# A new hand-set order for the 2,475 operations of a two-branch kernel (S4D convolution beside Hedgehog linear attention)

## The chip, the cores and the metric

The kernel runs on one core of a Trainium2 chip. Its time is the device time of one execution in microseconds (us). The engines are PE (TensorE: matrix products into PSUM), DVE (VectorE), ACT (ScalarE), POOL (GpSimd) and SP (SyncE, which issues all DMA transfers here). Each engine works through its own queue in order.

## The reference

Two independent branches read their own inputs, and their results stand side by side in the output (2048 rows, 576 + 576 columns).

```python
# A: S4D convolution.  u: 2048 x 576, 128 states per channel
dt = exp(log_dt);  A = -exp(log_A_real) + 1j * A_imag;  C = (C_real + 1j * C_imag) * dt
P = exp((A * dt)[:, :, None] * pos)                    # 576 x 128 x 2048
K = 2 * einsum("dn,dnl->dl", C, P).real                # the convolution's kernel
y = irfft(rfft(u, 4096) * rfft(K, 4096))[:2048] + u * D_skip
# B: linear attention, 32 heads of 18.  x: 2048 x 576
q, k, v = x @ wqkv;  pq, pk = q @ w_phi, k @ w_phi     # w_phi per head
phi = concat(softmax(p), softmax(-p))                  # for q and for k
o = phi_q (phi_k^T v) / (phi_q sum(phi_k) + 1e-6);  out = o @ wo
```

## The kernel before, in words

Branch A is a Fourier transform in two stages, written as small matrix products. Its steps are: `mags` and `par` (the parameters); 18 `group` units, each of two groups of 16 channels, which build the convolution's kernel; `kfirst` (first stage of the transform of the kernel, four quarters); `u` (the same for the input, 16 steps); 16 `product` units (second stage, product, and the first stage back); 16 `last` units (second stage back, and the stores). Between the stages the data goes through DRAM. A group's six PSUM tiles of sizes (step g0, PE) are exponentiated on ACT (L793), multiplied on DVE (L797 to L802), and enter the matmuls of step g4. In a product, p1 and p2 turn input and kernel on PE, DVE multiplies (L307), p3 adds on POOL or DVE, p4 turns back on PE, and two copies into `zo` buffers are stored.

Branch B folds w_phi into wq and wk (`fold`, 128 x 128 blocks), runs 16 `key` tiles of 128 rows (two products with 14 matmuls per half of the columns, softmax, and a sum over rows into one PSUM bank), turns the sum (`kv`), and runs 16 `query` tiles (product, softmax q1 and q2, transposes q3, division q4, transposes q5, product with wo q6, store). The first 8 tiles of x are kept in DRAM as `xd` by the key tiles, and loaded again by the query tiles (L400).

All operations are first recorded in `Plan.ops`, 2,475 of them, each with its engine. For some there are two engines ("any": ACT or DVE; others: POOL or DVE). `Plan.run` then emits them in the order of one list of numbers, `ORDER` (from L971). A number there can carry `x` (the other engine), `@` with the PSUM banks that the operation's new tiles take, and `:n`, which puts n matmuls of zeros (L230, 128 x 256, bf16) on PE ahead of it. Nothing else sets the order: each engine's queue is the list, cut down to that engine. An operation that has to wait (for data, for a free buffer, for a PSUM bank) holds up all that stands behind it in its queue, SP's DMAs too.

A buffer comes from a tag with a fixed number of places, given out in the order of the list. The tags that matter here: `zi`, `zo` and `v1` have 2 places, `e`, `x9`, `ot` and `ac` 3, `cs` and `ub` 5. PSUM has 8 banks, and the list says which one each tile takes; a tile of 576 columns takes two.

The places that the prediction speaks of: `load_again` (L400), the query tile's last product (step q6) and its store (L583), `product` (loads L886 and L877, stores L935), and `last`, whose load of `zi` or `cs` (L945) comes after the last store of all eight products of its half, and whose two stores (L958) free an `ot` buffer.

Of the kernel before, what the change touches and what calls it, by code (L numbers as in the profile page):

```python
# [971 lines left out]
0 1 2 4 3 5 1132 1136 1135 1124 1186 1133 34 1134 51 20 1137 35@0:26 36 39 52 21@2:10 22 37 53 1138 1139 1148 1140 1155 1141 1142 1143 1105 38 27 1144  # L972
1145 6 359 28@4 29 8@6 13 1146 32 40 1147 1149 7 25 23 1150 360 30 14@0:11 15 1106 1127 47 1151 1156 1193 44 361x 11 9 362 18 16 48 33 31 26 24 279
1152 1153 1157 1154 1158 1159 12 1160 1161 54 45 57@4 364@2 1024 1167 1168 41 1108 1128 280 1162 10 17 1163 19 363:2 1164 1109 1110 1107 49 42 281x
1035 56 376 299 1100 46 282x 1111 368 61 367 59@6 366@0 43 365 72 55 1095 1112 1125 58 1113 1116 370 1129 60 1118 369 1114 1115 371x 1117 377 1096@20
1120 62 63 1121 1122 300 70 64x 301x 73 1036@46 1098 65 284@0 1119 1037x 66 372 1126 373 1165 1166 1194 1187 1195 1188 1196 1189 1190 283 1097x 1197
1198 1038 1232 1191 74 1192 302 67 374 1123 288 287 1180 289 75x 68 306@4 375 303@6 1169 304 307 1224 177 1199 308 1201 1231 1233 1234 1090 1225 69
305 1235 1170 50@2 1226 71 378 317x 310 1179 1200 114 1099 1202 1183@30 309 1236 311 290 291 1428 1039 1203 286@4 77@6 1206 178 1171 1184@13 1204 1207
292 1212 78 293 1205 1429 1208 1215 285 1025 1030 1185@03 76 312 1209 82 1210@1 1227 1237 1228 1229 81 83 294 297 1431 179 316 115 180 182@4 181 183
1230 1238 1214 1211x 79@6 313 314 1213 1432 1218 116 117 80 295x 1172 84 1263 315x 318 186 187 1217 1216 188 1262 296 298 1173 1433 1219@3 1239 1240  # L980
85x 1221@10 1241 189 379 1269 1270 1271 1272 1264 91 1220x 1242 1244 339 340 1245 219 1181 118 86 1080 1182 119@4 90 1174 1175 1176 1430 184@6 341x
1222@31 342 198 1250 1243 1130 132 1177 1273 185 120 87 190x 1253 121@0 1178 1265 191 1274 1434 88 220 1435 124 89x 123 125 122 126 1223@45 1247 92
196 1251 1246 199 1248@3 221 1436 1437 222 133 1266 1308 1267 1252 195 127 224@6 223 1275 1268 128 1254 1256 192 1453 1452 1438 193 343@0 1249 129
1277 1276 1278 344 194x 1255 93 345@4 348 197 228 1439 130 346 227 347 229 1260@36 350 349 1281 1307 357 200 201x 1309 131x 1259@70 1279 1257@1 134
351x 1440 1441 230 226@4 94 1258 231 1288 1301 1300 1282 1285 1302 1303 95 1280 1283 1304 232 1444 225 1284 237 204@0 1305 233 203 1306 1314 96 395x
1291 1081@46 1286@3 236 1083 1082 234 235 238 1310 1261@67 352 208 207 209 210 1290 353 1289 1293 99@4 98 205@0 1311 354 1294 206 1312 1313 319 1292
1084 320 1315 211 1339 321 102 103 104 1338 356 1287 216 1316 355x 1050 1442 217 1101@64 1102x 1295@3 105 1297@01 1317 106 1340 1341 1342 1298@67 1318
97 202 1326 1346 1103x 1345 322 1296x 1320 100@4 101 1319 1323 1322 107 1070 1321 1329 259 260 1343 1344 358 1299@30 212 1352 1324@1 1347 1348 1349
1350 323@6 324 1328 108 109 1104 1351 111 110x 239 1327 1325x 112x 1331 1332 327 325@4 328 329 240 113 1443 1330 1445 261 262 1353 1071@06 326 1354
1072 1446 1073 1447 241x 213 1449 1448 242 1451 1091@06 330 337 1336@34 1092 1093 1045 1333@5 331x 1335@01 243@6 1450 214 1381 135 1454 244 1455 1456  # L990
1384 1457 1334 1074 1355 1358 156 1458 245@4 1459 1357 1361 1360 1527 1460 215x 1461 1356 1359 248 247 246 136 157 218 1362@3 249 1476 1131 257x 158
1462 332 264@0 1363 159x 1364 1365@64 1528 1529 1530 1531 263 333 1520 1482 336 1521 1522 1523 1524 1525 250 1483 256 334 1094 1366x 1367 1337@34 1368
1383 1382 268 267 251 1386 269 335x 270 1387 266@6 252 265 271 1369@04 338 1385 137 138 1370 1371 1388@3 1373@04 253 1475 1372 1374x 277 140@6 1375
1377@40 1376 1489 475 1065 272 273 274 1484 1532 1378x 141 1379x 254 1490 1491 1389x 145 144 162@4 146 161 160 1051@06 1533 1535 1526 1492 1485 1534
1486 1536 255x 276 1487 275x 258 1053 165 147 1518@36 1052x 1517@70 1537 1538 278 1054 166 168 167 396 1546 1540 142@4 1539 1541 143 1549 1075 1380
# [78 lines left out]
```

## Time and profile before

| | |
|---|---|
| median of 3 runs | 548.41 us (548.35 to 549.57) |
| the profiled execution's own time | 552.82 us |
| its span, first to last instruction | 551.0 us |
| mean granted PE clock | 0.990 |
| busy: PE, DVE, ACT, POOL | 529.0, 455.8, 378.6, 319.0 us |
| matmuls on PE | 8,048, of them 102 of zeros |
| DMA | 107.01 MB |

Rows of the profile read: line of the kernel, engine, operation, output<-inputs by the kernel's names, partitions x elements, count, and busy time with the mean of one in ns. A wait is put down to the instruction or transfer that ended it.

### The profile page before, as it was taken

The numbers are of one execution on the slowest core, as the hardware profiler recorded it, in microseconds if no ns is written. First come the engines' busy times: TensorE is split into PE (matmuls) and PEld (weight loads), VectorE is DVE, ScalarE is ACT, GpSimd is POOL, SyncE is SP. The second block draws the span as 40 slices with busy tenths as digits, with TensorE's granted clock in tenths as the row PEclk, the third lists the DMA queues.
The fourth block names the chain that finished last, engine by engine and source line by source line (L and its number), as shares of the span: only waits on it lengthen the run. The fifth ranks groups of instructions, "written<-read, shape, count | busy, mean of one in ns | idle before, by whom it ended". The sixth has DMA issues, their size and how long they took to land. (4 is left out here: it accounts for less than half of the span.)

```text
span 551.0 us, 18919 instructions
## 1 busy us (share of the span) xinstructions
PE 529.0 (96%) x8048; PEld 440.9 (80%) x8048; DVE 455.8 (83%) x762; ACT 378.6 (69%) x549; POOL 319.0 (58%) x463
## 2 busy tenths in 40 slices
PE   8999999999999889999999999978999999999997
PEld 7888999988988777888877577656879777777976
DVE  7999998979878889989999998978966878758541
ACT  4769849699468889899799987987732442533431
POOL 1645777964689877970888867884503544503200
PEclk9999999999999999999999999989799999999999
DMA  8858510263266568626662778555569788887876
GB/s 218 277 189 279 187 30 21 72 219 92 83 164 221 180 215 286 195 87 176 207 207 107 209 234 249 162 183 156 172 182 291 228 266 262 259 260 244 301 230 169
DMA packets 85650, 107.01 MB, mean 194 GB/s; under 512 B 5186, under 2 KB 69826, under 8 KB 85566
## 3 DMA queue, kind: packets, MB, share of 16 engines
q1 hardware_dynamic: 85566, 105.80, 61.6%
q8 instruction: 63, 1.03, 0.8%
q14 instruction: 21, 0.17, 0.1%
HBM read 61.24 MB, written 44.54 MB: 192 GB/s over the span
## 5 line engine op out<-in xcount | busy, mean ns | idle before, releaser
L288 PE MATMUL psum<-wh,x 128*128 128x288 f32 x576 | 123.3, 300 | 1.7 <-DMA x<-xd 0.9
L288 PE MATMUL psum<-vh,x 128*128 128x288 f32 x576 | 123.7, 302 | 1.2 <-DVE v L293 0.6
L739 POOL TENSOR_TENSOR cs<-cs,pi 128x64 int32<-128x64 int32 (+4 forms) x180 | 106.1, 596 | 9.2
L288 PEld LDWEIGHTS psum<-vh,x 128*128 128x128 f32 x576 | 94.9, 190 | 7.4 <-issue 2.9
L288 PEld LDWEIGHTS psum<-wh,x 128*128 128x128 f32 x576 | 94.2, 188 | 7.7 <-issue 2.6
L288 PE MATMUL psum<-vl,x 128*128 128x288 f32 x320 | 94.3, 297 | 0.5 <-DVE vl L376 0.5
L288 PE MATMUL psum<-wl,x 128*128 128x288 f32 x320 | 93.9, 296 | 0.1
L793 ACT ACTIVATE psum<-psum 128x512 f32<-128x512 f32 x108 | 59.0, 585 | 8.9 <-PE psum L288 8.4
L288 PEld LDWEIGHTS psum<-vl,x 128*128 128x128 f32 x320 | 60.9, 190 | 0.9 <-DVE vl L376 0.9
L288 PEld LDWEIGHTS psum<-wl,x 128*128 128x128 f32 x320 | 60.2, 188 | 0.3 <-DVE wl L360 0.3
L303 POOL TENSOR_TENSOR x<-zo,x 128x512 fp32r<-128x512 f32 (+1 forms) x34 | 31.6, 934 | 45.1 <-ACT x L387 31.6
L303 POOL TENSOR_TENSOR e<-e,small 128x1152 f32<-128x1152 f32 (+1 forms) x26 | 43.8, 1684 | 12.7 <-DVE small L307 5.6
L797 DVE TENSOR_TENSOR cs<-psum,cs 128x1024 f32<-128x1024 f32 x36 | 43.8, 1218 | 6.5 <-ACT psum L793 6.5
L288 PE MATMUL psum<-cs 128*32 128x64 f32 x2304 | 41.3, 223 | 4.5 <-issue 4.3
L798 DVE TENSOR_TENSOR cs<-psum,cs 128x1024 f32<-128x1024 f32 x36 | 43.7, 1214 | 1.2 <-ACT psum L793 0.8
L303 POOL TENSOR_TENSOR e<-small,e 128x576 f32<-128x576 f32 x22 | 25.7, 1170 | 32.5 <-DVE small L431 30.0
L288 PEld LDWEIGHTS psum<-cs 128*32 128x32 f32 x2304 | 35.0, 111 | 11.7 <-issue 7.7
L288 PE MATMUL psum<-ub,ff 64*32 64x288 f32 x1024 | 40.1, 418 | 2.5 <-ACT zo L293 0.9
L288 PEld LDWEIGHTS psum<-kvb,fT 126*128 126x128 f32 (+1 forms) x320 | 38.8, 190 | 4.6 <-issue 1.7
L293 ACT ACTIVATE zi<-psum 128x576 f32<-128x576 f32 x43 | 26.5, 651 | 23.2 <-PE psum L288 17.4
L434 ACT ACTIVATE e<-e 128x1152 f32<-128x1152 f32 x32 | 37.2, 1170 | 6.0 <-POOL e L303 4.8
L288 PE MATMUL psum<-kvb,fT 126*128 126x133 f32 (+1 forms) x320 | 41.2, 278 | 0.1
(153 smaller groups left out, 1128.3 us busy)
## 6 DMA issues: line engine op xcount, KB each, us to landing
dram<-zi SPq DMA_DIRECT2D x32, 576.0 KB, 7.2
ub<-dram SPq DMA_DIRECT2D x64, 288.0 KB, 4.0
dram<-zo SPq DMA_DIRECT2D x32, 288.0 KB, 4.4
zo<-in_xT_dram SPq DMA_DIRECT2D x24, 320.0 KB, 5.0
zi<-dram SPq DMA_DIRECT2D x12, 576.0 KB, 7.2
ub<-in_u_dram SPq DMA_DIRECT2D x16, 288.0 KB, 4.6
xd<-x SPq DMA_DIRECT2D x8, 576.0 KB, 5.2
x<-xd SPq DMA_DIRECT2D x8, 576.0 KB, 5.7
```

What stands on the lines that cost most here:

```text
L288: pe.matmul(o, l, r, start=start, stop=stop, skip_group_check=skip)
L293: op(("act", "dve"), (c_act(n), c_dve(n)), lambda e: act.activation(dst(), src(), AF.Copy) if e == "act" else dve.tensor_copy(dst(), src() ...
L303: op(eng, [c_dve(n[0]) if e == "dve" else c_pool(n[1]) for e in eng], lambda e: (dve if e == "dve" else pool).tensor_tensor(dst(), a(), b( ...
L434: op("act", c_act(1152) + 40, lambda: act.activation(e.t, e.t, AF.Exp), r=[e], w=[e], table="exp")
L739: op("pool", c_pool(2 * n * W), lambda n=n, j=j: pool.tensor_tensor(x()[:, :, :, n:2 * n], x()[:, :, :, 0:n], pi.t[:, j:j + 2, gs].bitcast ...
L793: op("act", c_act(512), lambda b=b: act.activation(b.t, b.t, AF.Exp), r=[b], w=[b], table="exp")
L797: op("dve", c_dve(64 * W), lambda: dve.tensor_tensor(F(), both(M.t), F(), op=ALU.mult), r=[M, cs], w=[cs])
L798: op("dve", c_dve(64 * W), lambda: dve.tensor_tensor(E.t[:, :, :, 32:64], both(up.t), cs.t[:, :, :, 0:32], op=ALU.mult), r=[up, cs], w=[E])
```

## The change

Only the list of numbers is new. The operations, their tiles, the tags and their places are the same. The first line of the list, before and now (89 such lines became 90):

```diff
 ORDER = """
-0 1 2 4 3 5 1132 1136 1135 1124 1186 1133 34 1134 51 20 1137 35@0:26 36 39 52 21@2:10 22 37 53 1138 1139 1148 1140 1155 1141 1142 1143 1105 38 27 1144
+0 1 2 4 3 1193 34 1132 1133 51 1135 5 35@0:13 36 39 20 21@2:22 27 1127 6 1124 22 359 1136 13 1134 1137 40 37 1138 1139 52 28@4 1140 1156 29 1141 38
...
```

Matmuls of zeros: 107 instead of 102. The start has 13 + 22 + 11 where it had 26 + 10 + 11, and a few stretches in the middle have some more or fewer. 163 operations run on their second engine instead of 160, so that DVE has one operation more, ACT two fewer, POOL one more. PE's operations are the same 481 with the same matmuls; most moves on PE are swaps of neighbours. On SP many transfers stand elsewhere. The lists also give other PSUM banks to many tiles.

Three places follow in detail. A number behind a name tells the buffers of one tag apart and differs between the two kernels.

The first is **SP's queue around the second load of x for query tile 6** (L400, `x9_4389` before, `x9_4200` now). Around it stand loads of the products (L886, L877), the stores of `u` (L608) and `kfirst` (L835), and the query tiles' result stores (L583; `ot_3912` before and `ot_3936` now are query tile 0's). Before:

```order
L886 DMA ub_4253<-dram_695 128x2x288
L886 DMA ub_4255<-dram_2390 128x2x288
L877 DMA ff_4376<-in_ff_dram 128x512
L886 DMA ub_4378<-dram_2390 128x2x288
L886 DMA ub_4380<-dram_695 128x2x288
L400 DMA x9_4389<-xd_863 128x1152
L583 DMA out_0_dram<-ot_3912 128x576
L886 DMA ub_4714<-dram_2390 128x2x288
```

Now:

```order
L400 DMA x9_3934<-xd_2845 128x1152
L835 DMA dram_2430<-zi_3948 128x8x144
L608 DMA dram_858<-zi_4025 128x1152
L583 DMA out_0_dram<-ot_3932 128x576
L400 DMA x9_4200<-xd_1091 128x1152
L608 DMA dram_858<-zi_4092 128x1152
L608 DMA dram_858<-zi_4113 128x1152
L583 DMA out_0_dram<-ot_3936 128x576
L877 DMA ff_4205<-in_ff_dram 128x512
```

The load stood behind the loads of the first products, and now stands ahead of all of them.

The second is **SP's queue in the last 30 us**. `zi_7885` before and `zi_7887` now are the load of `last` unit 12; `zi_7897` before and `zi_7810` now that of unit 8; `ot_7658` before and `ot_7651` now the result buffer of unit 1, whose second store stands here; the other `cs` and `zi` loads are those of other last units. Before:

```order
L958 DMA out_0_dram<-ot_7658 64x2x288
L945 DMA zi_7766<-dram_6780 128x1152
L958 DMA out_0_dram<-ot_7682 64x2x288
L945 DMA cs_7786<-dram_6780 128x1152
L945 DMA cs_7818<-dram_6780 128x1152
L945 DMA cs_7822<-dram_6780 128x1152
L958 DMA out_0_dram<-ot_7820 64x2x288
L583 DMA out_0_dram<-ot_7776 128x576
L958 DMA out_0_dram<-ot_7816 64x2x288
L945 DMA zi_7885<-dram_6780 128x1152
```

Now:

```order
L958 DMA out_0_dram<-ot_7673 64x2x288
L583 DMA out_0_dram<-ot_7783 128x576
L945 DMA cs_7808<-dram_6780 128x1152
L945 DMA zi_7810<-dram_6780 128x1152
L958 DMA out_0_dram<-ot_7651 64x2x288
L958 DMA out_0_dram<-ot_7856 64x2x288 x2
L945 DMA zi_7887<-dram_6780 128x1152
L583 DMA out_0_dram<-ot_7878 128x576
```

Unit 1's second store stood ahead of six of the eight loads of these units, and now stands behind seven of them. Ahead of it is unit 8's load, for which a `zi` buffer must come free.

The third is **PE's queue in the same stretch**: `zi_7766` before and `zi_7770` now is the input of last unit 10, the other `zi` that of unit 14; `o` belongs to query tile 14 and `fT` to 15; the last row is the first matmul of query tile 12's product with wo (`vh`), of which one half of the columns is done first. Before:

```order
L288 MATMUL psum_73<-zi_7766,w1_292 64x288 x4
L288 MATMUL psum_73<-zi_7759,w1_292 64x288 x4
L571 MATMUL psum_73<-ident_84,o_7764 128x128 x4
L572 MATMUL psum_73<-ident_84,o_7764 128x128
L288 MATMUL psum_73<-kvb_1048,fT_7788 128x133 x8
L288 MATMUL psum_73<-kvb_1048,fT_7788 128x76 x2
L288 MATMUL psum_73<-vh_3268,x9_7769 128x288
```

Now:

```order
L288 MATMUL psum_73<-zi_7762,w1_388 64x288 x4
L288 MATMUL psum_73<-zi_7770,w1_388 64x288 x4
L288 MATMUL psum_73<-kvb_896,fT_7801 128x133 x8
L288 MATMUL psum_73<-kvb_896,fT_7801 128x76 x2
L571 MATMUL psum_73<-ident_84,o_7781 128x128 x4
L572 MATMUL psum_73<-ident_84,o_7781 128x128
L288 MATMUL psum_73<-vh_3210,x9_7792 128x288
```

Units 10 and 14 have changed places, and the transposes went behind the division. In the list, query tile 12's product took the banks from 2 on before, in which unit 14 had its sums, and takes those from 0 on now, in which unit 10 has them.

More of the change, by code (lines that the diff above doesn't have):

```diff
@@ L976 @@
[L976 to L991, printed above, removed]
```

149 lines of the change are left out of this document (83 added, 66 removed).

## The prediction

> **What bounds the kernel now.** I began with the page's busy times and its slices.
>
> ```profile
> PE 529.0 (96%) x8048; PEld 440.9 (80%) x8048; DVE 455.8 (83%) x762; ACT 378.6 (69%) x549; POOL 319.0 (58%) x463
> PEclk9999999999999999999999999989799999999999
> ```
>
> PE is busy for 529.0 of 551.0 us, and the change leaves its matmuls as they are. Only three things can get shorter: the 22.0 us in which PE stands, what PE loses at a lowered clock, and the tail behind its last matmul. So I read what ended PE's waits (columns: us in total, times, longest).
>
> ```profile
> PE psum L288 <- issue: 4.3, 3, 2.4
> PE psum L288 <- ACT zi L293: 1.9, 2, 1.4
> ...
> PE psum L230 <- DVE zero L326: 1.5, 1, 1.5
> ...
> PE psum L288 <- DMA x<-xd: 0.9, 1, 0.9
> PE psum L288 <- DMA zi<-dram: 0.8, 1, 0.8
> PE psum L288 <- DVE v L293: 0.6, 1, 0.6
> ```
>
> There is no large wait: after the 4.3 us that are no wait for data ("issue"), each is at most 1.5 us. A new order can take away single ones of under a microsecond. Next the windows of 50 us around the places where it matters (busy us of PE, PEld, DVE, ACT, POOL, then the PE clock).
>
> ```profile
> 50.00:100.00 50.00, 50.00 (x885) 46.95 (x884) 46.40 (x70) 40.29 (x55) 39.92 (x55) 1.00 0.32 106
> ...
> 300.00:350.00 50.00, 48.59 (x954) 34.55 (x938) 47.48 (x73) 41.88 (x62) 38.53 (x58) 1.00 0.74 221
> 350.00:400.00 50.00, 44.53 (x861) 32.35 (x863) 43.65 (x63) 38.99 (x57) 33.30 (x49) 0.90 0.52 156
> ```
>
> From 50 to 100 us PE is never idle. From 300 to 350 us DVE is busy for 47.48 of 50 us, nearly as much as PE: a PE wait that an order takes away there can come back a little later, since DVE's work is the same. From 350 to 400 us the clock is 0.90, and there windows of 5 us show more.
>
> ```profile
> 365.00:370.00 5.00, 2.59 (x88) 1.36 (x82) 1.98 (x5) 4.47 (x6) 3.90 (x7) 0.90 0.51 163
> 370.00:375.00 5.00, 5.00 (x68) 3.32 (x52) 4.12 (x7) 3.10 (x4) 4.69 (x6) 0.76 0.40 114
> ...
> 385.00:390.00 5.00, 4.30 (x53) 2.96 (x55) 4.55 (x6) 3.56 (x8) 0.48 (x1) 0.61 0.96 290
> 390.00:395.00 5.00, 5.00 (x105) 4.43 (x100) 5.00 (x7) 4.19 (x8) 3.67 (x4) 0.71 0.72 217
> ```
>
> PE was busy for 2.59 of 5 us, and then had 0.90 and 0.76 of its clock; later 0.61 and 0.71. Lost clock: 5 x (0.10 + 0.24) = 1.7 us, and 5 x (0.39 + 0.29) = 3.4 us, 5.1 us in all.
>
> **The change part by part.** The sum is made against the profiled execution's 552.82 us (its span of 551.0 and 1.8 around it), and brought to the median by 548.41 / 552.82 = 0.992.
>
> *Waits removed.* In PE's timeline (start, length, and in brackets the idle time ahead):
>
> ```profile
> 48.85 0.40 PE L288 MATMUL psum<-vh,x 128*128 128x288 f32 x1 [0.64 <-DVE v L293]
> ...
> 50.79 0.30 PE L288 MATMUL psum<-wh,x 128*128 128x288 f32 x1
> ...
> 287.18 0.41 PE L288 MATMUL psum<-vh,x 128*128 128x288 f32 x1 [0.27 <-ACT ot L293]
> ...
> 290.17 0.37 PE L288 MATMUL psum<-wh,x 128*128 128x288 f32 x1 [0.86 <-DMA x<-xd]
> ...
> 310.65 1.35 PE L288 MATMUL psum<-ub,ff 64*32 64x288 f32 x32 [0.36 <-DVE o L307]
> 312.58 0.72 PE L288 MATMUL psum<-ub,ff 64*32 64x288 f32 x16 [0.57 <-ACT ac L293]
> ...
> 355.70 0.40 PE L288 MATMUL psum<-wh,x 128*128 128x288 f32 x1 [0.64 <-DVE ac L307]
> ...
> 534.53 1.19 PE L288 MATMUL psum<-zi,w 128*64 128x288 f32 x8 [0.80 <-DMA zi<-dram]
> ```
>
> And what such a load of x takes, from the DMA rows (KB, median us to landing):
>
> ```profile
> x<-xd SPq DMA_DIRECT2D x8, 576.0 KB, 5.7
> ```
>
> Query 6's product at 290.17 waited 0.86 us for x, a load of 5.7 us. The load now stands on SP ahead of all loads of the first products, for whose buffers it no longer waits; if that brings it forward by one such load, it is there in time. The same product also goes ahead of query 2's half (287.18), which had 0.27 us to wait for a bank. Removed: 1.13 us.
>
> The wait at 534.53 is `last` 12's, the load issued at 528.64 in the chain of waits:
>
> ```profile
> 527.93 0.61 SPq L958
> ...
> 528.64 5.76 DMA zi<-dram
> ...
> 547.31 0.65 ACT ot L293
> ```
>
> A `zi` load needs 5.76 us here. Unit 12 now comes after units 8, 11 and 15 as well on PE, where 9 alone was ahead of it; three more units of about 1 us (1.19 in the row at 534.53) against 0.80. Removed: 0.80 us.
>
> The key tile's product at 48.85 now has another key tile's half ahead of it (14 matmuls, 50.79 - 48.85 = 1.9 us), which covers its 0.64 us. At 355.70, query 8's first half waited 0.64 us for a bank; its second half now goes first, some 1.9 us of work. Removed: 0.64 each. Product 5's first stage (310.65, 312.58) waited 0.36 + 0.57 = 0.93 us; the third of its four turns takes another bank now, and its loads stand earlier, but one is still late by the same durations: removed 0.64 us, 0.3 left.
>
> Sum removed: 1.13 + 0.80 + 0.64 + 0.64 + 0.64 = 3.85 us. The last two (1.28) lie where DVE is nearly full; none of that need last, so the lower end is 2.6.
>
> *Waits added, the tail.* The DMA rows of the stores:
>
> ```profile
> dram<-zo SPq DMA_DIRECT2D x32, 288.0 KB, 4.4
> out_dram<-ot SPq DMA_DIRECT2D x32, 144.0 KB, 4.4
> ```
>
> Query 12's product now takes the banks of unit 10, whose copy needs the `ot` buffer of unit 1, whose second store now stands on SP behind unit 8's load, and that waits for unit 14's matmuls. From the end of those: the load's issue and the store's, 0.61 each by the chain's SPq row (the store's lies within its 4.4), 4.4 to land, 0.65 for the copy: about 5.7 us. PE has in between the other unit (about 1.1 us), query 15's division and query 14's transposes:
>
> ```profile
> 525.30 0.66 PE L571 MATMUL psum<-ident,o 128*128 128x128 f32 x4
> 525.80 0.27 PE L572 MATMUL psum<-ident,o 128*128 128x128 f32 x1
> 525.90 2.41 PE L288 MATMUL psum<-kvb,fT 126*128 126x133 f32 x20
> ```
>
> That is 1.1 + (528.12 - 525.30 =) 2.8, or 3.9 us. A stall of 1.3 to 1.8 us follows; nothing on PE can pass it. What it delays is everything to the end. Since SP's own wait may end earlier than I put it, the bounds are 0 and 1.8; I take 1.3. Behind the store on SP stand the other results' stores and unit 12's load, which has room (above).
>
> *Product 9's last step (448.87)* now takes the banks in which query 12's scores stood, and so for the last of DVE's three steps on those scores (maximum, minimum, addition):
>
> ```profile
> L307 DVE TENSOR_TENSOR e<-psum,small 128x576 f32<-128x576 f32 x32 | 24.0, 750 | 0.9 <-issue 0.5
> ```
>
> DVE has the list's order too, and the two preceding steps lie beside PE's work; bounds are 0 and one such step, 0.75, and since the step stands directly ahead of PE's in the list, I take 0.6.
>
> *Matmuls of zeros.* Five more.
>
> ```profile
> 1.46 5.73 PE L230 MATMUL psum<-ident,zero 128*128 128x256 bf16 x26 [1.46 <-DVE zero L326]
> 6.98 1.33 PE L288 MATMUL psum<-fT,kvb 72*128 72x72 f32 x10
> 8.15 1.26 PE L230 MATMUL psum<-ident,zero 128*128 128x256 bf16 x10
> 9.24 1.28 PE L288 MATMUL psum<-fT,cs 126*128 126x126 f32 x10
> ```
>
> One takes (9.24 - 8.15) / 10 = 0.109 us, and (6.98 - 1.46) / 26 = 0.212 us at the start, where the clock is still low. Five: 0.55 us, if they don't fall into a wait. The start itself: 13 cold ones end at 4.2 us, the first block, whose load now stands second on SP, takes 1.3 to 2, and 22 more, of which the last some 15 are warm, end near 9.2. Before it was 9.24 us: nothing.
>
> *Sum:* -3.85 + 1.3 + 0.6 + 0.55 = -1.4 us, from 552.82 to 551.4, and by 0.992 to **547.0 us**. With the ends named: -3.85 + 0.55 = -3.3 (545.1), and -2.6 + 1.8 + 0.75 + 0.55 = +0.5 (548.9).
>
> *What I leave at nothing:* the "issue" waits.
>
> ```profile
> q8 instruction: 63, 1.03, 0.8%
> ...
> 368.88 0.22 PE L288 MATMUL psum<-cs 128*32 128x64 f32 x1 [2.41 <-issue]
> ```
>
> 63 instruction packets for 8,048 matmuls and as many weight loads are one for every 255 or 256 of PE's instructions; the three waits stand 256 or a multiple apart in PE's count, in stretches of many small matmuls. Ten instructions more hardly move the marks: they still fall there, so the 2.41 us may grow, shrink or stay. The Trainium skill ("Runtime: NRT & Kernel Launch", Instruction fetch mechanics) says that an engine's instructions come in blocks of 256 and that crossing a border is mostly hidden. The count agrees with this trace, and the 2.41 us show a crossing that isn't hidden; by the rule alone 4.3 us would be a chance of this execution, and no order would owe them.
>
> **The rivals.**
>
> *More than the sum.* The idle 2.4 us before 369, and the low clock after it, may vanish together when the marks and the waits around 380 fall otherwise. Price: 2.41 of idle and 1.7 of clock at 369, less what DVE takes back, so about 3 us more: 551.4 - 3 = 548.4, by 0.992 **544.0 us**. For it: the clock needs only a little more work in one window. Against: 365 to 370 had ACT at 4.47 and POOL at 3.90 of 5 us, their work is the same, and the marks fall near the same place.
>
> *Slower: another low-clock window in 380 to 395.* Product 3's second result copy now needs the `zo` buffer of the first, whose store takes 4.4 us to land (above), since query 11's load of x took the other place. Query 6's last product takes that copy's bank. By these durations PE may wait up to 1.9 us longer at 388 to 391 than before. If PE then works for less than about half of such a window (2.59 of 5 us did it at 365), it has half its clock for another 3.4 us, 1.7 us lost. Price: 1.9 + 1.7 = 3.6, so 555.0, by 0.992 **550.6 us**. For it: 0.61 and 0.71 show this place on the edge already. Against: before, PE reached that product at 391 for other reasons, and the copy is ready near then, in which case the price is nothing. The Trainium skill ("TensorE: Matmul & The Clock Gate", Part 1: The HAM clock gate) says that the clock halves after an idle window of about 3.4 us and that these windows run freely. The 5.1 us worked out above for three of them agree (1.7 each); by its rule the phase differs between executions, and the start's 13 cold matmuls would warm the clock in some and not in others.
>
> *Nothing left.* The gains at 310 and 355 come back on DVE, and the tail costs its 1.8: the upper end, 548.4 to **548.9 us**. For it: the 47.48 of 50 us.
>
> *The change doesn't do what it says:* the removed waits were set by transfers that differ between executions (a load's 5.7 is a median), and the ones I named weren't there in the three timed runs. Then **548.4 us**.
>
> **How the numbers follow.** A difference under 0.3%, 1.65 us, can hardly be told from none for this kernel: faster means below 546.76, slower above 550.06. Chances: the sum 0.46 (a little under half of it below 546.76, its own range 545.1 to 548.9), more than the sum 0.20, slower 0.19, nothing left 0.10, not what it says 0.05. Faster: 0.20 + 0.21 = 0.41; slower: 0.19 + 0.02 = 0.21; no difference 0.38. The range goes from 543.6, the first rival with some more, to 550.6, the second.
>
> **What would show it.** The removed waits: no "DMA x<-xd" and no "DMA zi<-dram" among PE's waits, and no wait of 0.6 for "DVE v". The tail: PE's first `vh` matmul after query 14's transposes with an idle time of 1.3 to 1.8 us and ACT's `ot` copy ahead of it released by "DMA out_dram<-ot"; if there is no idle time there, the sum was 1.3 us too high. Clock: one low stretch at 369 and one at 386 to 393, with 5.1 us lost as before; a third makes the second rival, only one the first. A start in which the block after the 13 zeros waits for its load, or the clock is still low at 10 us, would make the forecast wrong, and so would waits in 100 to 300 us that I have put at nothing.

## The result: slower by 0.8%

| | before | the change |
|---|---|---|
| median, 5 runs each | 548.41 us (547.18 to 549.57) | 552.78 us (551.41 to 554.10) |
| ratio, 95% interval | | 1.0081 (1.0052 to 1.0109) |
| profiled execution: own time, span, clock | 552.82 us, 551.0 us, 0.990 | 552.49 us, 550.7 us, 0.994 |

The forecast was 547.0 us, so it has the wrong sign. By the two profiled executions alone the kernels would be level (552.82 and 552.49): the one of before lay 4.4 us over its own median, that of the change a little under its own. Any reading of two traces side by side has to reckon with that. The second pair of profiles (below) is no better in this: there the times are 550.36 and 549.50 us, and PE stands for 22.0 and 20.8 us in the two traces of the kernel before, and for 21.8 and 20.6 us in the two of the change. So the loss is not to be had as a difference of these traces; they show where waits went and came, and the timed runs show what that is worth. Seven executions in a slower state of the core (one of 553.49 us, six of 632 us and more, among these the only profiled one of the list with late loads) are left out of all figures.

The page of the changed kernel, busy times and PE's clock in 40 slices:

```profile
PE 528.9 (96%) x8053; PEld 440.9 (80%) x8053; DVE 460.3 (84%) x763; ACT 377.2 (68%) x547; POOL 319.2 (58%) x464
PEclk9999999999999989999999999999899999999999
```

PE is as busy as before. DVE has 4.5 us more (455.8 before) for one instruction more. Part of that is that the list also chooses engines: 57 operations carry an `x` only in the new list and 54 only in the old one, so that 111 operations run on another engine, though the counts (163 and 160) nearly agree. Another part stands in groups with as many operations of the same shape as before; these follow below.

What ended PE's waits in the changed kernel (us in total, times, longest):

```profile
PE psum L288 <- DMA ub<-dram: 2.3, 2, 1.7
PE psum L288 <- ACT zi L293: 2.1, 3, 1.4
PE psum L288 <- issue: 1.8, 1, 1.8
PE psum L230 <- DVE zero L326: 1.5, 1, 1.5
PE psum L288 <- DVE e L307: 1.4, 2, 1.2
...
PE psum L543 <- DVE e L307: 0.7, 1, 0.7
```

Three rows of these are new or much larger: "DMA ub<-dram" and "L543 <- DVE e L307" were not among PE's waits before, and "L288 <- DVE e L307" stood there with 0.2 us. (Smaller new ones, such as "DMA mg<-gd" and "DMA cs<-in_wkT_dram" with 0.7 us each, are not shown.) The rows "DMA x<-xd", "DMA zi<-dram" and "DVE v L293", which the forecast wanted gone, are gone. So most of the old waits went and others came. Their places, in PE's timeline:

```profile
230.44 1.65 PE L288 MATMUL psum<-kvb,fT 126*128 126x133 f32 x12 [1.21 <-DVE e L307]
...
245.16 0.85 PE L543 MATMUL psum<-ident,e 128*72 128x128 f32 x6 [0.66 <-DVE e L307]
...
291.21 0.40 PE L288 MATMUL psum<-wh,x 128*128 128x288 f32 x1 [0.15 <-ACT ot L293]
...
314.19 0.27 PE L230 MATMUL psum<-ident,zero 64*32 64x256 bf16 x1 [0.24 <-DVE ac L307]
315.13 2.05 PE L288 MATMUL psum<-ub,ff 64*32 64x288 f32 x48 [0.67 <-DMA ub<-dram]
...
462.97 1.21 PE L288 MATMUL psum<-ub,ff 64*32 64x288 f32 x32 [1.67 <-DMA ub<-dram]
```

The row at 291 is the place where 1.13 us stood before, and those at 314 and 315 are product 5's, where 0.93 us stood and 0.24 + 0.67 = 0.91 us stand now. Those at 230, 245 and 463 are places of which the forecast says nothing.

**The first new wait: DVE beside POOL.** Two groups of tiny operations take longer, though there are as many of them on DVE as before: those on the tile `small` 5.5 us in place of 3.3, those on `ks` 2.4 in place of 1.0. Their instructions, first of the kernel before and then of the change (shortest/median/longest in ns):

```profile
L307 DVE TENSOR_TENSOR small<-small x16: 130/192/421, 221.2 to 517.0; 128x32 f32<-128x32 f32 x16
L307 DVE TENSOR_TENSOR ks<-ks,dsk x4: 185/194/390, 147.3 to 401.6; 128x36 f32<-128x36 f32 x4
```

```profile
L307 DVE TENSOR_TENSOR small<-small x16: 121/182/2231, 223.6 to 517.9; 128x32 f32<-128x32 f32 x16
L307 DVE TENSOR_TENSOR ks<-ks,dsk x4: 197/494/1189, 147.2 to 401.7; 128x36 f32<-128x36 f32 x4
```

The median of the first group is nearly the same, its longest is 2.23 us where it was 0.42. A third group, the products' subtractions, has grown by 3.1 us, more than either; before, and in the change (busy us, mean ns, idle us ahead):

```profile
L303 DVE TENSOR_TENSOR ac<-ac 128x288 f32<-128x288 f32 x16 | 7.8, 520 | 0.1
```

```profile
L303 DVE TENSOR_TENSOR ac<-ac 128x288 f32<-128x288 f32 x16 | 10.9, 698 | 0.1
```

One of them takes 1.50 us at 483.50, where the shortest takes 0.38, beside a POOL operation on 128 x 576 that had started 0.12 us ahead; the kernel before has one of 1.55 us too. All of these stand behind 318 us, and no run here moves them by themselves. The two long ones of the first two groups, with what POOL was doing, in the timelines of DVE and POOL of the change:

```profile
225.68 2.36 POOL L376 TENSOR_TENSOR vl<-e,vh 128x960 fp32r<-128x960 f32 x1
...
225.86 2.23 DVE L307 TENSOR_TENSOR small<-small 128x32 f32<-128x32 f32 x1
...
241.76 1.17 POOL L303 TENSOR_TENSOR e<-e,small 128x576 f32<-128x576 f32 x1 [0.70 <-DVE small L307]
...
241.79 1.19 DVE L307 TENSOR_TENSOR ks<-ks,dsk 128x36 f32<-128x36 f32 x1
```

and the same operations in another execution of the kernel before:

```profile
225.89 0.18 DVE L307 TENSOR_TENSOR small<-small 128x32 f32<-128x32 f32 x1
...
227.32 2.22 POOL L376 TENSOR_TENSOR vl<-e,vh 128x960 fp32r<-128x960 f32 x1
...
239.81 0.18 DVE L307 TENSOR_TENSOR ks<-ks,dsk 128x36 f32<-128x36 f32 x1
...
240.04 1.17 POOL L303 TENSOR_TENSOR e<-e,small 128x576 f32<-128x576 f32 x1 [1.20 <-DVE ks L307]
```

In the change POOL's operation starts 0.18 us ahead of DVE's and ends at 225.68 + 2.36 = 228.04; DVE's ends at 225.86 + 2.23 = 228.09. At 242 it is 242.93 and 242.98. Both times DVE's operation ends 0.05 us behind POOL's, though by itself it takes a small part of that. Before, DVE's came first and took 0.18 us both times. Both inputs of these DVE operations are in SBUF. The Trainium skill ("SBUF — State Buffer", Who interferes with whom) says that a DVE instruction with two SBUF inputs contends with a GpSimd instruction that reads SBUF, that the shared port pair is an exclusive lock, and that issue order and not the shape of the operation decides who blocks. The trace agrees, with 0.18 us in the one order and 2.23 us in the other.

PE's wait at 230.44 is for the addition that takes a query tile's scores out of their PSUM bank. DVE's queue in the change behind the blocked operation:

```profile
225.86 2.23 DVE L307 TENSOR_TENSOR small<-small 128x32 f32<-128x32 f32 x1
228.01 0.75 DVE L428 TENSOR_REDUCE small<-psum 128x32 f32<-128x576 f32 x1
228.68 0.74 DVE L427 TENSOR_REDUCE small<-psum 128x32 f32<-128x576 f32 x1
229.45 0.22 DVE L431 TENSOR_REDUCE small<-small 128x32 f32<-128x64 f32 x1
229.63 0.76 DVE L307 TENSOR_TENSOR e<-psum,small 128x576 f32<-128x576 f32 x1
```

It ends at 230.39, PE goes on at 230.44. With 2.0 us less in the first row, and these rows as close behind one another as they are, PE's wait of 1.21 us would not be there.

**The second new wait: loads on SP.** SP's timeline in the change ahead of PE's wait at 462.97:

```profile
453.80 0.36 SPq L886 DMA_DIRECT2D ub<-dram  x1
454.21 1.59 SPq L958 DMA_DIRECT2D out_dram<-ot  x1
455.86 0.59 SPq L877 DMA_DIRECT2D ff<-in_ff_dram  x1
456.55 1.42 SPq L886 DMA_DIRECT2D ub<-dram  x3
```

The last row ends with loads of product 15, at 457.97. Ahead of them now stand product 13's load and the second store of last unit 4, which holds SP for 1.59 us where such an issue otherwise takes about 0.6 (0.61 in the prediction's chain of waits). The order belongs to the list, the long issue does not: in the change's second execution the same store holds SP for 0.61 us, and PE waits 0.41 + 0.38 = 0.79 us for the same loads.

### The profile page after: what moved, and what is told of

It is laid out like the page before. It is cut to its first block, busy times and chain, and to the rows that moved or that the text cites. A ratio compares the mean times of both kernels' runs of the same rounds, so it can differ in the third digit from the quotient of the medians.

```text
span 550.7 us, 18934 instructions
## 1 busy us (share of the span) xinstructions
PE 528.9 (96%) x8053; PEld 440.9 (80%) x8053; DVE 460.3 (84%) x763; ACT 377.2 (68%) x547; POOL 319.2 (58%) x464
## 4 chain that ended last, share of the span: by engine, by line
PE 42%; DVE 9%; DMA 4%; ACT 2%; issue 1%; SPq 1%; DVEq 0%; ACTq 0%
PE psum L288 38%; PE psum L543 3%; DVE cs L798 1%; PE psum L571 1%; DVE cs L797 1%; DVE ac L307 1%; DMA mg<-gd 1%; DMA dram<-zi 1%; DMA ub<-dram 1%; DVE cs L800 1%; DVE cs L802 1%; DMA ff<-in_ff_dram 1%; DVE small L427 0%; SPq L886 0%; DVE e L307 0%
## 5 line engine op out<-in xcount | busy, mean ns | idle before, releaser
L288 PE MATMUL psum<-wh,x 128*128 128x288 f32 x576 | 125.3, 304 | 0.4 <-ACT zi L293 0.2
L288 PE MATMUL psum<-vh,x 128*128 128x288 f32 x576 | 123.3, 301 | 0.2 <-DVE e L307 0.2
L739 POOL TENSOR_TENSOR cs<-cs,pi 128x128 int32<-128x128 int32 (+4 forms) x180 | 106.3, 600 | 7.5
L288 PEld LDWEIGHTS psum<-wh,x 128*128 128x128 f32 x576 | 95.2, 190 | 7.2 <-issue 3.1
L288 PEld LDWEIGHTS psum<-vh,x 128*128 128x128 f32 x576 | 94.1, 188 | 6.5 <-issue 3.3
L288 PE MATMUL psum<-wl,x 128*128 128x288 f32 x320 | 94.5, 297 | 0.1
L288 PE MATMUL psum<-vl,x 128*128 128x288 f32 x320 | 93.7, 295 | 0.8 <-DVE vl L376 0.8
L288 PEld LDWEIGHTS psum<-vl,x 128*128 128x128 f32 x320 | 60.6, 189 | 1.0 <-DVE vl L376 1.0
L288 PEld LDWEIGHTS psum<-wl,x 128*128 128x128 f32 x320 | 60.9, 190 | 0.4 <-DVE wl L360 0.3
L303 POOL TENSOR_TENSOR e<-e,small 128x576 f32<-128x576 f32 (+1 forms) x29 | 49.0, 1689 | 16.6 <-DVE small L444 8.4
L303 POOL TENSOR_TENSOR x<-zo,x 64x128 fp32r<-64x128 f32 (+1 forms) x35 | 30.2, 869 | 28.5 <-ACT x L387 27.5
L288 PEld LDWEIGHTS psum<-cs 128*32 128x32 f32 x2304 | 34.8, 111 | 11.1 <-issue 6.7
L288 PEld LDWEIGHTS psum<-kvb,fT 126*128 126x128 f32 (+1 forms) x320 | 38.8, 189 | 6.0 <-DVE e L307 2.1
L288 PE MATMUL psum<-cs 128*32 128x64 f32 x2304 | 40.7, 223 | 2.5 <-issue 1.8
L288 PE MATMUL psum<-kvb,fT 126*128 126x133 f32 (+1 forms) x320 | 41.5, 278 | 1.2 <-DVE e L307 1.2
L288 PE MATMUL psum<-ub,ff 64*32 64x288 f32 x1024 | 39.1, 409 | 3.5 <-DMA ub<-dram 2.3
L303 POOL TENSOR_TENSOR ac<-ac 128x288 f32<-128x288 f32 x32 | 26.1, 830 | 25.2 <-DVE ac L307 22.9
L293 ACT ACTIVATE zi<-psum 128x576 f32<-128x576 f32 x39 | 24.2, 650 | 23.0 <-PE psum L288 19.7
```

What stands on the lines that cost most here:

```text
L288: pe.matmul(o, l, r, start=start, stop=stop, skip_group_check=skip)
L293: op(("act", "dve"), (c_act(n), c_dve(n)), lambda e: act.activation(dst(), src(), AF.Copy) if e == "act" else dve.tensor_copy(dst(), src() ...
L303: op(eng, [c_dve(n[0]) if e == "dve" else c_pool(n[1]) for e in eng], lambda e: (dve if e == "dve" else pool).tensor_tensor(dst(), a(), b( ...
L739: op("pool", c_pool(2 * n * W), lambda n=n, j=j: pool.tensor_tensor(x()[:, :, :, n:2 * n], x()[:, :, :, 0:n], pi.t[:, j:j + 2, gs].bitcast ...
```

## The experiments

All kernels here use the same operations, and only the list differs. Each was timed next to the kernel before on the same chip; ratios are to that, with their 95% intervals.

### The same two kernels once more

The question was what belongs to the list and what to one execution.

> The kernel before, unchanged. Theory A: the profiled execution of before that the prediction was worked out from (552.82 us) was not an ordinary one; its two low-clock stretches (369 and 386 to 393 us, 5.1 us lost) and the 2.41 us stall for instructions are not in every execution. Then a new profile lies at 547 to 549.5 us, its clock is 0.99 or more in 350 to 400 us, and PE reaches the work of 200 us as before but that of 390 us some 4 us sooner. Theory B: profiling itself costs 4 us in this kernel; then the new profile has its own time near 552 to 553 us again, with the low clock in the same places, while the timed runs stay at 548.4.

> The changed kernel, unchanged. Theory A: its low-clock stretch at 203 to 206 us behind a 1.8 us stall for instructions is part of its ordinary execution (five timed runs all had a mean clock of 0.993 or 0.994); the new profile shows it again at the same place, and the time is 551.4 to 554.1 us, ratio 1.006 to 1.010. Theory B (the place of the low clock depends on the phase of free-running windows): the stretch is elsewhere or missing, and the time goes down by about 1.7 us for each one that is missing.

| | ratio | median us |
|---|---|---|
| kernel before, unchanged | 0.9990 (0.9966 to 1.0013) | 547.69 |
| the change, unchanged | 1.0087 (1.0057 to 1.0116) | 552.50 |

The loss stands. The kernel before came out in between its two theories: its second profiled execution has 550.36 us, without the 2.41 us of "issue", but again with a low clock in 350 to 400 us (0.93). In the change, where the clock is low does not belong to the list. The windows of 50 us (PE's clock is the third number from the end), first of the change:

```profile
200.00:250.00 50.00, 45.29 (x615) 39.12 (x603) 43.05 (x83) 42.37 (x61) 36.53 (x53) 0.97 0.54 174
350.00:400.00 50.00, 47.50 (x949) 35.11 (x953) 48.27 (x69) 44.18 (x63) 34.23 (x52) 0.97 0.63 190
```

then of the change run again:

```profile
200.00:250.00 50.00, 46.73 (x643) 39.69 (x644) 46.09 (x90) 44.88 (x65) 38.84 (x55) 1.00 0.56 186
350.00:400.00 50.00, 46.74 (x969) 34.14 (x971) 48.15 (x72) 42.94 (x62) 33.29 (x49) 1.00 0.61 181
```

The same list lost 3% of the clock in two such windows in one execution and nothing in the other. The 1.8 us of "issue" at 202.54 in the first is 0.16 us in the second, and the 2.41 us at 368.88 that the prediction quotes of the kernel before isn't there when that kernel runs again. As the baseline of all these experiments the kernel before went from 544.5 to 553.3 us (126 executions, mean 548.1, standard deviation 1.5).

### Where in the list the loss lies

Lists were spliced: the first n words of one list, and then all other operations in the other's order.

```diff
-ORDER = before
+ORDER = now[:812] + [the other operations in the order of before]    # to 188 us
+ORDER = now[:1183] + ...                                             # to 260 us
+ORDER = now[:1626] + ...                                             # to 342 us
+ORDER = now[:1935] + ...                                             # to 407 us
```

> The new list for its first 812 operations (PE's first 188 us: both folds, all key tiles, half of the groups), then the old list's order for what is left. The whole change costs 4.8 us (552.5 against 547.7). Theory START (the start's loads and zeros): most of it is here, 551 to 552.5 us. Theory MIDDLE (188 to 400 us, where DVE is full and PE has single waits): 547 to 548.5 us here. Theory END (waits for the products' loads at 461 us and the stores and loads of the last 140 us): 547 to 548.5 us too.

> The new list for its first 1,183 operations (to 260 us of PE), then the old order. START: 551 to 552.5 us, as to 188 us. MIDDLE, if it is the stretch of the first query tiles, where the changed kernel's first profile lost 5 us against the old one's: 550.5 to 552.5 us. MIDDLE, later: 548 to 549. END: 547 to 548.5 us.

> The new list for its first 1,626 operations (to 342 us of PE), then the old order. MIDDLE by the first query tiles or by the first products: 551 to 553 us. MIDDLE by the last groups (342 to 400 us) or END: 547.5 to 549 us.

> The new list for its first 1,935 operations (to 407 us of PE), then the old order, in which the last eight products, seven query tiles and all but three of the last units lie. START and MIDDLE: 551.5 to 553 us, all of the loss. END: 547 to 549 us, and the old tail gives the loss back.

| new order up to | ratio | median us |
|---|---|---|
| 188 us | 1.0015 (0.9995 to 1.0036) | 548.61 |
| 260 us | 1.0064 (1.0042 to 1.0086) | 551.47 |
| 342 us | 1.0040 (1.0014 to 1.0066) | 550.68 |
| 407 us | 1.0073 (1.0046 to 1.0100) | 552.12 |
| all (run again) | 1.0087 (1.0057 to 1.0116) | 552.50 |

The two lists put their matmuls of zeros at different places, so that the splices here and below have 98 to 111 of them. At 0.109 us each (from the prediction) this is, as an estimate, at most 1.0 us away from the 102 of the kernel before. A step of 0.5% lies between 188 and 260 us, where the first new wait is. The others are smaller than the intervals. The same from the other side:

```diff
-ORDER = before
+ORDER = before[:1176] + [the other operations in the order of now]           # new from 260 us
+ORDER = before[:1935] + ...                                                  # new from 407 us
+ORDER = before[:1176] + [now, to 407 us] + [before]                          # new from 260 to 407 us alone
```

> The old list for its first 1,176 operations (to 260 us of PE), then the new order. By subtraction from the run with the new list to 260 us (1.0064 of 1.0087): ratio 1.001 to 1.004, if the parts add up. The profile should show the waits at 290, 310, 489 and 534 us of the kernel before gone. If the second half alone costs nothing or gains (ratio under 1.001), the loss before 260 us is all there is. If it costs 1.006 or more, the parts don't add up, and the list loses by what each part leaves the other.

> The old list to 407 us, then the new order: the last eight products, seven query tiles and last units. Theory END (the load for product 15's step p2 at 461 us is late by 0.6 to 1.9 us in the changed kernel, and this varies with the memory): ratio 1.002 to 1.004. Rival: the removed waits at 489 and 534 us (1.1 and 0.5 to 1.0) balance it, ratio 0.998 to 1.001.

> The old list with the new order only from operation 1,176 to 1,935 (260 to 407 us of PE). In this stretch the forecast's removed waits at 287, 290, 310, 312 and 355 us lie. Theory TWO PLACES (the loss is in 188 to 260 us and behind 407 us; between them the new order gains what the forecast said): ratio 0.996 to 0.999. Theory ANY PIECE (every departure from the old list costs, since its near-ties had been settled on the chip): ratio 1.001 to 1.004.

| new order | ratio | median us |
|---|---|---|
| from 260 us on | 1.0044 (1.0019 to 1.0068) | 550.75 |
| from 407 us on | 1.0057 (1.0032 to 1.0081) | 551.31 |
| 260 to 407 us alone | 1.0011 (0.9990 to 1.0033) | 549.02 |

There is a second loss behind 407 us, and none that is clear of the noise between 260 and 407. The theory of two places had asked for a gain there, 0.996 to 0.999, and that did not come. More than half of the waits to be removed lie in that middle stretch (query 6, product 5, query 8: 1.13 + 0.64 + 0.64 of 3.85 us). The parts, 0.64% up to 260 us and 0.57% from 407 us on, make 1.2% where the change has 0.8 to 0.9%; with these intervals that is no clear difference. But a splice has a seam, at which one list's buffers and queues meet the other's, and the seam can cost something itself: at the seam of 407 us PE waits 0.96 us in two of these kernels and 0.82 us in the third, at a place where neither list by itself has a wait. Without it the middle stretch alone would be at about 0.9994, as an estimate from 0.96 us of 549, which is still short of the 2.41 us.

The next two set the stretch from 188 to 260 us alone, new in the old list, and old in the new list.

```diff
-ORDER = before
+ORDER = before[:821] + [now, to 260 us] + [before]
-ORDER = now
+ORDER = now[:812] + [before, to 260 us] + [now]
```

> The old list with the new order only from operation 821 to 1,183 (188 to 260 us of PE). TWO PLACES: ratio 1.0035 to 1.006, about half of the loss, with PE's waits for DVE at 230 and 245 us in the profile. ANY PIECE or the start's part needed as well: 1.001 to 1.003.

> The new list with the old order only from operation 812 to 1,176 (188 to 260 us of PE). TWO PLACES: 1.003 to 1.005, about half of the loss left, that behind 407 us. If the waits there are shifted and not removed (as with the two operations moved back): 1.007 to 1.009.

The first took 1.0085 (1.0048 to 1.0122), 554.0 us, the second 1.0061 (1.0033 to 1.0088), 551.24 us. The first is no clean measure: PE's timeline has 4.26 us of waits right at its seam, where the lists themselves have one of 1.44 us.

```profile
190.25 0.31 PE L288 MATMUL psum<-cs 128*32 128x64 f32 x4 [3.04 <-issue]
...
192.34 0.79 PE L288 MATMUL psum<-sel,mg 64*128 64x512 f32 x2 [1.22 <-DVE zi L293]
```

In the second the waits at 230 and 245 us are gone, and its seams show none above the lists' own (1.32 us at 190 in place of 1.44 at 192). It comes out 0.26% lower than the change, a difference within the two intervals.

### The two operations at 226 and 242 us

Here the two suspected pairs are moved by themselves: 436 is POOL's `vl` (L376), 1593 is DVE's `ks` (L307). DVE's `small` operation is 487, which stands ahead of 488 in both lists. First the new list, with both put back into the order in which DVE's goes first:

```diff
 1591@0 455 1592
-436
 1391@60:5 549 548
 ...
 1392@54 1412 488
+436
 1698 460@2 1419
 ...
 1731 1079 469
+1593
 557 1732
-1593
 495@7 558 514
```

> The new list with two operations moved: POOL's subtraction of 128 x 960 (L376) behind the multiplication that it had overtaken, and DVE's addition of the skip term (128 x 36, L307) two places forward on DVE. In every profile with the new list to 260 us, a DVE operation of 128 x 32 beside that subtraction takes 2.22 us, and the 128 x 36 one 1.19 us beside a POOL multiplication; with the old list they take 0.17 and 0.18. PE then waits 1.25 and 0.73 us for DVE. Theory DVE BESIDE POOL: both durations fall below 0.25 us in the profile, both PE waits go, and the time falls by 1.3 to 2.5 us, to about 550 to 551 (ratio to before 1.004 to 1.007). Theory ELSEWHERE (the waits move on, or the loss is in DMA and the clock): the time stays at 551.8 to 553 (1.008 or more).

It took 1.0086 (1.0057 to 1.0116), 552.56 us: no gain. The trace shows where the wait went (timelines of DVE, POOL, ACT and PE of this kernel):

```profile
225.09 0.18 DVE L307 TENSOR_TENSOR small<-small 128x32 f32<-128x32 f32 x1
...
228.79 2.23 POOL L376 TENSOR_TENSOR vl<-e,vh 128x960 fp32r<-128x960 f32 x1
...
231.24 1.16 POOL L303 TENSOR_TENSOR e<-small,e 128x576 f32<-128x576 f32 x1
...
232.43 1.17 ACT L434 ACTIVATE e<-e 128x1152 f32<-128x1152 f32 x1 [2.53 <-POOL e L303]
...
234.43 0.66 PE L543 MATMUL psum<-ident,e 128*126 128x128 f32 x4 [1.70 <-ACT fT L293]
```

Both DVE operations take 0.18 to 0.19 us again, and the waits at 230 and 245 are gone. But POOL's 2.23 us now stand ahead of its subtraction for query tile 3, ACT's exponential waits 2.53 us for that, and a copy which frees a PSUM bank for PE stands behind the exponential on ACT. PE waits 1.70 us at 234.43 in place of 1.21 + 0.66 = 1.87 us. The wait has moved.

Then the old list, in which only these two are moved the wrong way round:

```diff
 1590 1411 453
+436
 456@4:6 454@6 1085
 ...
 1592 459x 551
-436
 1392@41:5 1727 1391@67
 ...
 467 1705 511
-1593
 1620 1614 468
+1593
 558 1621 1622
```

> The old list with the opposite edit: POOL's subtraction of 128 x 960 (L376) ahead of the multiplication, and DVE's addition of the skip term one place back. DVE BESIDE POOL: the 128 x 32 operation takes 2 us and more, the other about 1 us, PE waits for DVE at 229 and about 241 us, and the time rises by 1 to 2.5 us, ratio 1.002 to 1.0045. ELSEWHERE: ratio 0.999 to 1.0015.

It took 1.0060 (1.0036 to 1.0085), 550.96 us: two words of 2,475 cost about 3 us, more than expected. In its trace (POOL, DVE, PE):

```profile
223.20 2.23 POOL L376 TENSOR_TENSOR vl<-e,vh 128x960 fp32r<-128x960 f32 x1
...
224.66 0.83 DVE L307 TENSOR_TENSOR small<-small 128x32 f32<-128x32 f32 x1
...
228.14 0.50 PE L288 MATMUL psum<-sel,mg 64*128 64x512 f32 x1 [1.12 <-DVE fT L293]
```

POOL's ends at 225.43, DVE's at 225.49, and PE has a wait of 1.12 us where the traces with the old order there have 0 to 0.46. The blocked operation explains 0.83 - 0.18 = 0.65 us of it. The `ks` operation took 0.85 us, and PE had no wait for it. So the order of such a pair costs time in the old list, and in the new one it is entangled with the rest of the stretch: putting the pair right alone brings nothing back. What part of the 3 us is the blocking itself is not shown, for the move also sets POOL's multiplication, which was first, behind 2.23 us of other work. Another 0.60 + 0.58 us of waits for DVE stand at 396 and 398 us, behind a load for which ACT waits 1.22 us; whether the moved pair makes that load late is not shown either.

### The loads of product 15

The new list, with the loads of product 15 (2373, 2374, 2380, 2381) ahead of product 13's load (2331) and last unit 4's store (2418):

```diff
 2297 2301x 773
+2373 2374 2381 2380
 2331 2418
-2373 2374
 857@2 831 858
 ...
 2376@4 2378@6 832x
-2381 2380
 2262 2414 2419
```

> The new list with four loads of product 15 ahead of one load of product 13 and one store on SP, where the old list has them. In five profiles with the new order there, PE waits 0.6 to 2.0 us (mean 1.25) for product 15's step p2 at about 461 us; in seven with the old order it does not wait. TWO PLACES with this as its second half: that wait is gone, and the time falls by about 1.2 us, ratio 1.0055 to 1.0075. If another load is late instead: 1.008 or more, with a new wait for a product's load between 450 and 480 us.

It took 1.0043 (1.0022 to 1.0064), 550.74 us, where the change beside the same kind of baseline has 1.0087. SP's timeline in this kernel:

```profile
454.32 2.31 SPq L886 DMA_DIRECT2D ub<-dram  x4
456.68 0.61 SPq L958 DMA_DIRECT2D out_dram<-ot  x1
```

The store goes behind the loads, takes 0.61 us, and PE has no wait for "ub<-dram" between 455 and 467 us. In the six profiles with the new order here that wait is there, with 0.8 to 2.1 us (1.4 in the mean), and in none of the nine with the old order. About 2.4 us of the loss (0.0044, with an uncertainty of about 0.0036 from the two intervals) hang on these four loads behind a load and a store; the wait itself is 1.4 of them.

The counter-test makes the loads late in the old list:

```diff
 2288@4 2262 2291
+2331
 2373 2374
-2380
 916 917 2429
 ...
-2381
 831@0 830 832x 2376@2 2378@6
+2381 2380
 2261
-2331
 2384@4 2377x 774
```

> The old list with the opposite edit behind 407 us: product 13's load ahead of product 15's, and product 15's last two loads where the new list has them. Nothing else changes. LOADS: a PE wait of 0.6 to 2 us at 461 us with the releaser DMA ub<-dram, and ratio 1.001 to 1.004. If the wait at 461 us needs the rest of the new order: ratio 0.999 to 1.001 and no wait.

1.0005 (0.9988 to 1.0022), 548.49 us: it costs nothing. This order of the loads alone is not enough. That the old list has slack at that place, which the new order behind 407 us doesn't have, would explain it, but no trace here shows whether PE waited in this kernel, and what would have taken the slack was not tried.

### Both mended

The new list with the old order from 188 to 260 us, and with product 15's loads first: the last two edits in one.

> The new list with the old order in 188 to 260 us and with product 15's four loads first on SP as well: both suspected places mended. TWO PLACES: ratio 1.000 to 1.0035 (one mend alone gave 1.0061, the other 1.0043, of 1.0087). If the two mends overlap, or a third place costs: 1.004 to 1.006.

1.0052 (1.0021 to 1.0082), 551.87 us: no better than the loads alone, and by its expectation a sign that the two mends overlap or that a third place costs. The new waits are gone (PE's longest wait in 186 to 264 us is 1.57 us of "issue"; none at 230, 245 or 463), but this list runs at a lower clock: 0.9916 in the mean of its 8 executions, where the kernel before has 0.9957 over all of its own. If all time went as the clock, that would be (0.9957 - 0.9916) x 550 = 2.3 of its 2.9 us, as an upper estimate: its own executions go from 546.62 us at 1.000 to 551.72 to 553.09 at 0.988, but those of the kernel before at 0.999 or more have a mean of 547.9 us, hardly below the 548.1 of all. Its profiled execution has the loss at two places:

```profile
200.00:250.00 50.00, 47.96 (x645) 41.37 (x648) 44.44 (x87) 44.83 (x68) 37.69 (x55) 0.97 0.51 169
...
350.00:400.00 50.00, 46.84 (x884) 35.05 (x872) 46.15 (x66) 42.63 (x61) 33.13 (x51) 0.93 0.61 184
```

Executions in which hardly any clock was lost (0.999 or more) can be put side by side:

| | executions at such a clock | their times, us |
|---|---|---|
| kernel before, as baseline | 23 of 126 | 545.9 to 550.4, mean 547.9 |
| the change | 2 of 14 | 549.50, 550.49 |
| old order from 188 to 260 us | 1 of 11 | 549.32 |
| loads of product 15 first | 2 of 12 | 548.50, 548.85 |
| both mended | 1 of 8 | 546.62 |

They go down in the order that the two suspected places ask for, and the last is level with the kernel before. One or two executions each are a hint and no proof. Why the doubly mended list has the lower clock stays open, and so does the rival that its expectations name, that every larger departure from the old list costs something. No run separates the order from the 111 engines and the PSUM banks that changed with it. No list tried here is faster than the kernel before.

## Why the prediction was wrong

It said -3.85 us of waits removed, +2.45 added, and 547.0 us. Point by point:

**Most of the waits it named went, and that was nearly worthless.** Query 6's 0.86 + 0.27 us are 0.15; "DMA zi<-dram" (0.80, and only 0.33 when the kernel before runs again) is gone, and so is the key tile's 0.64 (in the second profile of the change there are 0.37 us nearby); query 8's 0.64 is gone at its place, with a wait of 0.5 us for DVE some microseconds behind it in both profiles. Product 5's did not go: 0.93 us are 0.24 + 0.67 in the one profile and 0.24 + 0.75 in the other, now for its loads, so that the 0.64 us of that term were not there to be had. The stretch that holds the waits of query 6, product 5 and query 8 measures 1.0011 (0.9990 to 1.0033) when it alone is new, where 2.41 us less would be 0.996. That agrees with the warning beside the sum, that a PE wait taken away there can come back a little later; it was given to two of the terms only, and should have been given to all three of that stretch.

**The step that failed** is the one that was not in the sum: "waits in 100 to 300 us that I have put at nothing". The forecast looked at the places where a wait stood before, and asked whether it goes. It looked at three places where the list makes new ones. The two that the runs found were elsewhere: 188 to 260 us (1.0015 to 1.0064 in the splices), with PE waits of 1.21 and 0.66 us for DVE, and the loads of product 15, behind even those 300 us (a wait of 1.67 us; 1.0087 to 1.0043 when they go first). For the first it took each operation's duration as fixed, and DVE operations of 0.18 us took 2.23 and 1.19. The row of the tile `small` in the profile of before, with 421 ns as the longest against a median of 192, already showed that a duration isn't fixed: that operation, at 292.05 us, ended 0.04 us behind a POOL operation that had started ahead of it. With both places put right the list still measures 1.0052, so these two are not shown to be the whole of the loss, and the rest stays open.

**SP's queue was read at the wrong place.** The prediction followed SP at 290 us and in the last 30 us. The same question, what now stands ahead of a load and how long SP holds there, asked of every product would have found a load and a store put ahead of product 15's loads, though not that the store's issue would take 1.59 us in one execution.

**The tail stall of 1.3 us didn't come.** PE, ACT and SP of the change at that place:

```profile
525.50 4.96 SPq L958 DMA_DIRECT2D out_dram<-ot  x2
...
525.99 2.52 PE L288 MATMUL psum<-kvb,fT 126*128 126x133 f32 x20
...
526.25 0.65 ACT L293 ACTIVATE ot<-psum 128x576 f32<-128x576 f32 x1 [1.32 <-PE psum L288]
...
528.81 0.38 PE L288 MATMUL psum<-vh,x 128*128 128x288 f32 x1
```

Unit 10's copy ran at 526.25, released by PE's matmuls, while unit 1's store was issued from 525.50 on, and a store of that size takes some microseconds to land:

```profile
out_dram<-ot SPq DMA_DIRECT2D x32, 144.0 KB, 2.7
```

So the copy can't have waited for that store's buffer, and must have had another of the three places. That the places go round strictly in the list's order was an assumption, and it was wrong here. PE's product follows at 528.81 without idle time. The median landing of such a store is 2.7 us in both profiles of the change, and 4.4 and 5.1 in the two of the kernel before: a landing time taken from one list does not hold for another.

**Product 9's last step** (0.6 us) had no wait: DVE's addition ended at 448.00, and PE reached the step at 448.62. Both false additions (1.9 us) made the forecast slower than its own gains, so without them it would have been further off.

**Start and issue waits.** The start was as forecast: 13 matmuls of zeros, the block, 22 more, and 0.7 us for a load behind them. That no order owes the "issue" waits was right: the mark that cost 1.80 us cost 0.16 in the next execution of the same kernel.

**The time base was weak.** 552.82 us held 5.1 us of lost clock and 2.41 us of "issue" by chance. Multiplying the sum by 0.992 corrects the mean, but it hides that another execution has other stalls than the trace that was searched for them: in the second profile of the kernel before the 2.41 us are gone, and PE stands 1.2 us less in all.

**The rivals.** "Slower: another low-clock window in 380 to 395" has the sign, but not the mechanism: PE waits 0.35 us at 388.86 in the change, and 0.75 at that place when it runs again, where that rival asked for up to 1.9; and the second time the clock is 1.00 in that stretch and the execution takes 549.50 us all the same, where the kernel before has 547.9 in the mean at such a clock. "More than the sum" rested on the 2.4 us at 369, which the kernel before itself doesn't have when it runs again.

## What to carry to other kernels

When only an order changes, don't only ask which old waits go: for each engine, look at which pairs of instructions now run at the same time, above all a short DVE operation with both inputs in SBUF that now starts just behind a long POOL operation, and at what now stands ahead of each load on the queue that issues it. In a group of instructions read the longest beside the median; a longest of twice the median can be a duration that depends on the neighbours. Before a sum of terms under a microsecond is made on one trace, see where that execution stands among the kernel's own times, and try a suspected pair in both lists: one whose wrong order costs 0.6% in the old list gave nothing back when it was put right in the new one.

## What the runs showed of the hardware

A DVE operation on 128 x 32 values took 0.18 us, or 0.83 and 2.23 us when a POOL operation that reads SBUF had started before it: it lasted until POOL's ended, to within 0.06 us, in each of the cases shown. PE's "issue" wait at one and the same place of the list was 1.80 us in one execution and 0.16 in the next, and the granted clock of one and the same list was 0.994 and 1.000 in the mean, with low stretches at 200 to 210 us and 385 to 395 us in the one and at neither in the other. One and the same store held SP for 1.59 us in one execution and 0.61 in the other.
